# Blocks of 16 for the first three triangular inverses, joined by 32x32 products, and the norm products at another place in the later slots

## The chip, the cores and the metric

The kernel runs on one core of a Trainium2 chip. The metric is device time in microseconds (us) for one execution. The engines named here are TensorE (PE: matmuls; PEld: its weight loads), VectorE (DVE), ScalarE (ACT), GpSimd (POOL) and SyncE (SP). SP does no arithmetic; it issues DMA transfers in the order of its program, as POOL and ACT also do between their other instructions.

## The reference

Two blocks in a row. The first is a recurrence over 768 tokens for 4 x 8 heads with a 40 x 40 state each; the second is a feed-forward block with a softmax-weighted activation and a layer norm.

```python
for t in range(S):
    kt, vt, rt = (k[:, :, t], v[:, :, t], r[:, :, t])
    wt, at, bt = (w[:, :, t], a[:, :, t], b[:, :, t])
    y[:, :, t] = np.einsum('bhd,bhde->bhe', rt, state)
    Sa = np.einsum('bhde,bhe->bhd', state, at)
    state_decay = state * wt[:, :, None, :] - np.einsum('bhd,bhe->bhde', Sa, bt)
    state = state_decay + np.einsum('bhd,bhe->bhde', vt, kt)
...
h = x @ w_in
e = np.exp(h - h_max)
solu = h * (e / (np.sum(e, axis=-1, keepdims=True) + 1e-09))
ln = (solu - mu) / np.sqrt(var + 1e-06) * g_ln
out = ln @ w_out
```

Shapes: r, k, v, w, a, b are (4, 8, 768, 40) in float32; x is (3072, 320); w_in is (320, 1024) and w_out (1024, 320), both delivered in 64 bits and turned into float32 on the chip.

## The kernel before

The 768 tokens are cut into chunks of 64 (C), and two batches are worked on together, so there are 24 chunk steps i (N), each with 16 units (p, q, g, h) of one batch and head. Within a chunk the recurrence becomes products plus one triangular system per unit: a strictly triangular 64x64 matrix nt (line 383) has to be inverted as identity plus triangle. The kernel keeps two 32x32 diagonal blocks (Q = 32) of each and inverts them on VectorE; the off-diagonal block follows from two products on TensorE.

The inverse of two chunks (GRP = 2, so 32 units, 128 partitions with one block each) is one generator, `invert(n)` (line 402). `spread` (393) first reads the blocks back from a DRAM copy of nt into the tile blk. Then come 30 steps of forward substitution, each with one multiply (L415, prod) and one subtract (L417, uu) on VectorE. At the end the result is stored to DRAM (L422), and `bring(i)` (426) loads it in two arrangements: tu and uh. `flip` (438) transposes tu on VectorE, and `couple` (444, product py) and `close` (457, product pz) form the off-diagonal block.

The order of work is written out by hand for PE, POOL, DVE and SP; each of these engines runs its list in that order. The main loop (785) is a pipeline. One turn of it, called slot i here, starts at -1 and works on several chunks at once: the solution and output of chunk i (`driven`, `solved`, `answered`, `read`, `leave`), the preparation of chunk i+1 (`attend_kv`, `attend_rs`, `scores`, `couple`, `close`), `front`, `norm` and `scaled` of chunk j = i+5 and its neighbours, and the feed-forward block of earlier chunks (`hidden`, `exped`, `weighed`, `folded`, `output`). The steps of inverses are laid between these by `some(k)`, which advances the oldest inverse by k steps; the table `shares` (783) gives k for four places of a slot, and `narrowed` (784) says how many conversions of a weight part from 64 bits (`split`, 174: five VectorE and three ScalarE instructions) stand in the first and the second half of a slot. Ahead of the loop, chunks 0 to 3 pass through `front` and `norm`, inverse 0 is begun after chunk 1 and inverse 1 after chunk 3.

Names used below. nt is the masked product pnt of `norm`; psi and lv are the two masks of the product ps in `scores` (L505, L506, both recorded as L362); nmax (L655) is the row maximum with which the softmax chain begins; x and tot (L604, L619) are written by `leave`; kb is the scaled key tile on POOL (L329), and pb its transposition on TensorE; xT is the transposed activation that `leave` and `left` move by DMA on SP and POOL. Loads issued by `load_keys` and `load_values` go to SP unless another queue is given.

In slot i, TensorE's list runs: px (chunk i), pa, pb (chunk j), pu, pk, pv (chunk i+1), pnt (chunk j), pr, pst (chunk i+1), the last part of h, pei, pl, pcum, ps, py, pz, pyo.

Of the kernel before, what the change touches and what calls it, by code (L numbers as in the profile page):

```python
# [17 lines left out]
P = 128  # L18
# [4 lines left out]
AHEAD = 5  # L23
LANDS_NEXT = {2: 6, 3: 7, 5: 8, 6: 9, 7: 10, 8: 11, 10: 12}
LAG = 1
LN_EXP = "natural_log_exp_and_others"


def shape_constants():
    s, t = np.arange(P)[:, None], np.arange(P)[None, :]  # L30
    same = s // C == t // C
    row = np.arange(P)[:, None] % C
    parts = dict(
        ident=np.eye(P),
        cum=same & (s <= t),
        tri=row < np.arange(C)[None, :],
        eye_hi=row == Q + np.arange(Q)[None, :],
        neg_hi=-(row >= Q).astype(np.float64),
        mean=np.full((P, P), 2.0 ** -10),
    )  # L40
    at, where = 0, {}
    for name, x in parts.items():
        where[name] = (at, at + x.shape[1])
        at += x.shape[1]
    return np.concatenate([np.asarray(x, np.float64) for x in parts.values()], 1).astype(np.float32), where
# [3 lines left out]
def kernel(  # L49
# [46 lines left out]
    def c_(name):  # L96
        lo, hi = where[name]
        return cst[:, lo:hi]
# [8 lines left out]
    def zeroed(engine, name, shape, n, part=None):  # L107
        tiles = []
        for i in range(n):
            x = const.tile(shape, FP32, name=f"{name}{i}")  # L110
            engine.memset(x if part is None else part(x), 0.0)
            tiles.append(x)
        return tiles
# [10 lines left out]
    st_t = zeroed(nc.vector, "st", [P, 8, C], NPAIR)  # L124
    tu_t = zeroed(nc.vector, "tu", [P, H, 3 * Q], 2)
    uh_t = zeroed(nc.vector, "uh", [P, 2 * H, Q], 2)
    x0 = zeroed(nc.vector, "x", [P, 2, 4, C], 1, lambda x: x[:, :, :, D:])[0]
    wy = const.tile([P, 2, 4, C], FP32, name="wy")
    nc.vector.tensor_copy(out=wy.rearrange("p h j c -> p (h j) c")[:, :, Q:],
# [127 lines left out]
    def fence():  # L257
        nc.tensor.drain()
# [20 lines left out]
    def ok(i):  # L279
        return 0 <= i < N  # L280


    def load_keys(i, names, queue=nc.sync):
        if not ok(i):
            return
        for n, ap in (("w", w), ("b", b), ("a", a), ("k", k)):
            if n in names:
                x = a_t[i % 4] if n == "a" else two.tile([P, H, D], FP32, tag="raw_" + n, name="raw_" + n,
                                                             bufs=3)
                st[i]["raw_" + n] = x  # L290
                load(x, ap, i, queue)

# [80 lines left out]
    def norm(i):  # L373
        if not ok(i):
            return
        d = st[i]
        t = banks("pnt")
        for u in in_turn(lambda p, q, g, h: (h, p ^ h)):
            p, q, g, h = u
            j = 2 * q + g  # L380
            mm(t[half(p ^ h), h, j * C:j * C + C], keyed(d["bT"], u), keyed(d["aT"], u))
        nt = d["nt"] = tokens("nt", AHEAD)
        masked(nt, t[:, :, 0:256])
        n, at = divmod(i, GRP)
        if at == 0:
            blocks[n] = dram.tile([2 * GRP * H, C, C], FP32, tag="nt_dram", name="nt_dram")
        queue = nc.sync if i < 4 else nc.gpsimd
        queue.dma_start(out=blocks[n].rearrange("(a h x) s c -> a x s h c", a=GRP, x=2)[at].rearrange("x s h c -> (x s) h c"),  # L388
                          in_=nt.rearrange("p h j c -> p (h j) c"))
# [3 lines left out]
    def spread(n):  # L393
# [5 lines left out]
                queue.dma_start(out=nb[home:home + Q], in_=blocks[n][:, Q * e:Q * e + Q, Q * e:Q * e + Q])  # L399
        return nb  # L400

    def invert(n):
        nb = spread(n)
        yield
        u = two.tile([P, Q // 2, Q], FP32, tag="uu", name="uu")
        flat = u.rearrange("p c t -> p (c t)")
        nc.vector.memset(u[C:P], 0.0)
        nc.vector.memset(flat[C:P, 1::Q + 2], 1.0)
        nc.vector.tensor_scalar(out=u[0:C], in0=nb[0:C, 0::2], scalar1=-1.0, scalar2=None, op0=ALU.mult)
        nc.vector.memset(flat[0:C, 0::Q + 2], 1.0)  # L410
        for j in range(1, Q - 1):
            m, n_c = Q - 1 - j, (j + 1) // 2
            prod = two.tile([P, Q * Q // 8], FP32, tag="prod", name="prod", bufs=1)
            t = prod[:, 0:n_c * m].rearrange("p (c r) -> p c r", c=n_c)
            nc.vector.tensor_tensor(out=t, in0=nb[:, j:j + 1, j + 1:Q].to_broadcast([P, n_c, m]),  # L415
                                    in1=u[:, 0:n_c, j:j + 1].to_broadcast([P, n_c, m]), op=ALU.mult)
            nc.vector.tensor_tensor(out=u[:, 0:n_c, j + 1:Q], in0=u[:, 0:n_c, j + 1:Q], in1=t, op=ALU.subtract)  # L417
            if j < Q - 2:
                yield
        inverse[n] = dram.tile([C, Q, Q], FP32, tag="uu_dram", name="uu_dram")  # L420
        for y in range(2):
            nc.sync.dma_start(out=inverse[n][:, y::2], in_=u[C * y:C * y + C])  # L422
        yield


    def bring(i):
        if not ok(i):
            return
        d = st[i]
        d["tu"], d["uh"] = tu_t[i % 2], uh_t[i % 2]  # L430
        n, at = divmod(i, GRP)
        src = inverse[n].rearrange("(e a h x) c t -> e a h x c t", e=2, a=GRP, x=2)
        for x in range(2):
            nc.sync.dma_start(out=d["tu"][C * x:C * x + Q, :, Q:2 * Q], in_=src[0, at, :, x].rearrange("h c t -> c h t"))
        for x in range(2):
            nc.sync.dma_start(out=d["uh"][C * x + Q:C * x + C], in_=src[1, at].rearrange("h x c t -> c (h x) t"))

    def flip(i):
        if not ok(i):
# [273 lines left out]
    def some(n):  # L713
        while steps and n:
            if next(steps[0], steps) is steps:
                steps.pop(0)
            else:
                n -= 1
# [1 line left out]
    parts = ((n, part) for n in range(len(lands) + NF) for part in landed[n])  # L720

    def begin_inverse(n):
        steps.append(invert(n))
        next(steps[-1])


# [10 lines left out]
    for i in range(4):  # L737
        scaled(i, "b")
        if i == 3:
            scaled(0, "k")  # L740
            scaled(1, "k")
        front(i)
        decay(i + 1)
        norm(i)
        decay_turned(i + 1)
        if i == 0:
            load_keys(2, "ba")
        if i == 1:
            load_keys(3, "w")
            begin_inverse(0)  # L750
            narrow(2)
            load_keys(3, "ba")
            load_keys(0, "k")
            load_keys(4, "w")
            some(8)
        if i == 2:
            load_values(0)
            load_keys(1, "k")
            some(8)
    load_keys(5, "w")  # L760
    load_keys(4, "ba")
    begin_inverse(1)
    for i in (2, 3):
        load_keys(i, "k", nc.gpsimd)
# [5 lines left out]
    decay(5)  # L770
    load_keys(6, "w")
    land(3, nc.sync)
    some(14)
    load_keys(5, "ba")
    load_values(1)
    bring(0)
    bring(1)
    load_keys(5, "k")
    for n in (4, len(lands)):
        land(n, nc.sync)  # L780


    shares = {-1: (0, 6, 2, 6), 0: (0, 6, 4, 6), 1: (0, 6, 3, 6), 2: (0, 6, 3, 6), 3: (0, 6, 3, 6)}
    narrowed = {-1: (0, 1), 0: (1, 1), 1: (1, 2), 2: (1, 2), 3: (1, 1)}
    for i in range(-1, N + 3 + LAG):
        j, m = i + AHEAD, i - LAG
        pieces = shares.get(i, (3, 6, 0, 6))
        some_weights = narrowed.get(i, (0, 0))

        some(pieces[0])  # L790
        if i >= 1:
            bring(i + 1)
        if i >= 0:
            load_values(i + 2)
        carried(i)
        driven(i)
        front(j)
        hidden(m - 2, ((0, 1),))
        if i == 3 + LAG:
            centred(mean, 6)  # L800
        load_keys(j + 3, "w")
        load_keys(j + 2, "bak")
        narrow(some_weights[0], pieces[1])

        solved(i)
        attend_kv(i + 1)
        hidden(m - 2, ((1, 1),))
        norm(j)
        attend_rs(i + 1)
        hidden(m - 2, ((2, 0), (2, 1)))  # L810
        exped(m - 2)
        decay_turned(j + 1)
        scaled(j + 1)
        left(i - 1)

        answered(i)
        if i >= 0:
            flip(i + 1)
        weighed(m - 2)
        spreadof(m - 2)  # L820
        decay(j + 2)
        if i == 0:
            turn_g()
        if i == 2 + LAG:
            mean = mean_begun(6)
        output(m - 3, 0)
        if ok(j) and j % GRP == GRP - 1:
            begin_inverse(j // GRP)
        some(pieces[2])
        scores(i + 1)  # L830
        if i < 0:
            flip(i + 1)
        couple(i + 1)
        output(m - 3, 1)
        narrow(some_weights[1], pieces[3])

        close(i + 1)
        read(i, True)
        read(i, False)
        by_value(i + 2)  # L840
        leave(i)
        folded(m - 2)
        hidden(m - 1, ((0, 0), (1, 0)))
# [30 lines left out]
```

## Time and profile before

| what | value |
|---|---|
| time, median of 3 runs | 638.88 us (638.88 to 640.07) |
| the profiled execution, its own time | 639.79 us |
| its span in the profile | 637.7 us |
| mean granted TensorE clock | 0.93 |
| PE busy | 567.5 us (89%), 11451 instructions |
| DVE busy | 461.9 us (72%), 1286 instructions |
| ACT busy | 245.3 us (38%) |
| POOL busy | 269.1 us (42%) |
| L415 (prod), 360 instructions | 99.0 us, 275 ns each |
| L417 (uu), 360 instructions | 101.9 us, 283 ns each |
| chain that ended last, by engine | PE 71%, DVE 13%, DMA 6%, issue 4% |

The 360 steps belong to the twelve inverses. A float32 product shows as two weight loads and two matmuls in the records, which is why the counts there are twice those of the program. Busy time is the time in which an engine has an instruction running; a matmul's end is modelled, so its pace is better read from the starts of a series. The chain that ended last goes back from the last instruction, at each step to what released it.

### The profile page before, as it was taken

Reading aid. Unit: us, or ns where it says so; the run is one execution under the profiler, and the core shown is the slowest. Engines: PE = TensorE matmul, PEld = TensorE weight load, DVE = VectorE, ACT = ScalarE, POOL = GpSimd, SP = SyncE. Lnnn points to the kernel's source line nnn. Section 1 sums busy time; section 2 is a strip of 40 time slices with the busy share of each in tenths; the row PEclk is TensorE's granted clock in tenths of the full one; section 3 lists DMA queues with packets and bytes.
Section 4 is the critical chain, followed back from the end, with each engine's and each line's share of the span. In section 5 each row is a group of like instructions: output and inputs, shape, how many; then the busy total and the mean of one; then the engine's idle time right before and its main releaser. Section 6 shows DMA issues by size and latency. Waiting matters only on the chain.

```text
span 637.7 us, 26729 instructions
## 1 busy us (share of the span) xinstructions
PE 567.5 (89%) x11451; PEld 399.6 (63%) x11451; DVE 461.9 (72%) x1286; ACT 245.3 (38%) x498; POOL 269.1 (42%) x444
## 2 busy tenths in 40 slices
PE   5245677988999999999999999999999999999995
PEld 3134555756577677667667767666776666766653
DVE  4678799999878778778878777787887796443431
ACT  3412545554334434433443443344243333332221
POOL 3334345574274444445543642743544642222200
PEclk9665676688999999999999999999999999999998
DMA  8939896474355535544554553654423422210000
GB/s 166 159 73 169 170 164 131 107 152 87 71 110 93 111 87 95 107 93 103 103 120 79 108 116 73 119 107 95 91 53 70 98 49 49 51 36 26 24 20 21
DMA packets 217868, 59.92 MB, mean 94 GB/s; under 512 B 203216, under 2 KB 213048, under 8 KB 217752
## 3 DMA queue, kind: packets, MB, share of 16 engines
q1 hardware_dynamic: 200984, 34.47, 31.7%
q0 software_dynamic: 11376, 19.25, 12.6%
q10 hardware_dynamic: 5392, 4.51, 2.5%
q8 instruction: 90, 1.47, 1.0%
q14 instruction: 26, 0.21, 0.1%
HBM read 40.10 MB, written 13.37 MB: 84 GB/s over the span
## 4 chain that ended last, share of the span: by engine, by line
PE 71%; DVE 13%; DMA 6%; issue 4%; ACT 2%; SPq 2%; POOL 1%; DVEq 0%; ACTq 0%; POOLq 0%
PE h L254 16%; PE po L703 14%; PE pyo L254 7%; PE px L254 4%; PE pu L254 3%; DVE uu L417 3%; PE plnT L692 3%; PE ps L254 3%; DVE prod L415 3%; PE pl L254 2%; PE pr L334 2%; PE pnt L254 2%; PE pk L334 2%; PE pa L334 2%; PE pz L254 2%
## 5 line engine op out<-in xcount | busy, mean ns | idle before, releaser
L254 PE MATMUL h<-w_in,xT 128*128 128x512 f32 (+1 forms) x288 | 121.6, 614 | 0.0
L415 DVE TENSOR_TENSOR prod<-blk,uu 128x30 f32<-128x30 f32 (+4 forms) x360 | 99.0, 275 | 24.0 <-DMA blk<-nt_dram 14.0
L703 PE MATMUL po<-w,lnT 128*128 128x320 f32 x384 | 113.5, 440 | 0.0
L417 DVE TENSOR_TENSOR uu<-uu,prod 128x30 f32<-128x30 f32 (+4 forms) x360 | 101.9, 283 | 12.4
L703 PEld LDWEIGHTS po<-w,lnT 128*128 128x128 f32 x384 | 70.5, 190 | 29.3 <-issue 2.3
L655 DVE TENSOR_REDUCE nmax<-h 128x1 f32<-128x1024 f32 x24 | 29.4, 1224 | 60.0 <-PE h L254 59.9
L388 POOL DMA_DIRECT2D nt_dram<-nt x20 | 18.3, 916 | 119.0 <-DVE nt L362 97.7
L254 PEld LDWEIGHTS h<-w_in,xT 128*128 128x128 f32 (+1 forms) x288 | 38.9, 190 | 21.9 <-issue 20.8
L623 POOL TENSOR_TENSOR st<-tot,ex 104x160 f32<-104x160 f32 x44 | 22.1, 520 | 70.4 <-DVE tot L619 68.2
L681 POOL TENSOR_TENSOR rs<-c,mhalf 128x1 f32<-128x1 f32 x24 | 13.4, 559 | 91.0 <-DVE c L680 89.6
L635 POOL DMA_DIRECT2D xT<-x x96 | 48.7, 512 | 0.0
L254 PE MATMUL pyo<-lv,kb 64*64 64x104 f32 x768 | 38.6, 274 | 6.0 <-DVE lv L362 3.3
L693 ACT COPY lnT<-plnT 128x512 f32<-128x512 f32 x48 | 26.1, 589 | 43.3 <-PE plnT L692 43.3
L399 POOL DMA_DIRECT2D blk<-nt_dram x42 | 33.3, 800 | 13.0 <-DMA nt_dram<-nt 12.7
L658 ACT ACTIVATE e<-h,nmax 128x1024 f32<-128x1024 f32 x24 | 26.8, 1115 | 28.6 <-DVE nmax L655 27.5
L254 PE MATMUL pyo<-lu,kb 64*64 64x104 f32 x768 | 37.2, 266 | 0.0
L664 DVE TENSOR_TENSOR e<-h,e 128x1024 f32<-128x1024 f32 x24 | 29.4, 1225 | 10.1 <-ACT e L658 10.1
L276 POOL DMA_DIRECT2D raw_r<-in_r_dram x48 | 34.9, 729 | 0.3 <-issue 0.3
L672 DVE BATCH_NORM_STATS2 bs<-e 128x6 f32<-128x512 f32 x48 | 30.9, 686 | 0.8
L707 ACT ACTIVATE osb<-po,rs 128x320 f32<-128x320 f32 x24 | 12.7, 528 | 48.5 <-PE po L703 29.6
L254 PEld LDWEIGHTS pnt<-aT,bT 40*64 40x64 f32 x768 | 14.6, 144 | 26.5 <-issue 25.0
L254 PEld LDWEIGHTS pyo<-lv,kb 64*64 64x64 f32 x768 | 23.9, 145 | 11.3 <-issue 7.7
(130 smaller groups left out, 1127.0 us busy)
## 6 DMA issues: line engine op xcount, KB each, us to landing
blk<-nt_dram POOLq DMA_DIRECT2D x42, 128.0 KB, 4.2
nt_dram<-nt POOLq DMA_DIRECT2D x20, 256.0 KB, 3.5
raw_w<-in_w_dram SPq DMA_DIRECT2D x48, 80.0 KB
a<-in_a_dram SPq DMA_DIRECT2D x48, 80.0 KB
raw_r<-in_r_dram POOLq DMA_DIRECT2D x48, 80.0 KB, 3.3
lv<-in_v_dram SPq DMA_DIRECT2D x48, 80.0 KB
out_dram<-osb ACTq DMA_DIRECT2D x24, 160.0 KB
raw_b<-in_b_dram SPq DMA_DIRECT2D x44, 80.0 KB
```

What stands on the lines that cost most here:

```text
L254: nc.tensor.matmul(o, lhsT=lhsT, rhs=rhs, start=start, stop=stop, skip_group_check=True)
L276: queue.dma_start(out=x[half(p), :, 0:D], in_=ap[2 * bp + p, :, ci * C:(ci + 1) * C, :].rearrange("h t d -> t h d"))
L334: nc.tensor.transpose(out=t[0:W2, j * P:(j + 1) * P], in_=x[:, 2 * j:2 * j + 2].rearrange("p a b -> p (a b)")[:, 0:W2], identity=ident)
L399: queue.dma_start(out=nb[home:home + Q], in_=blocks[n][:, Q * e:Q * e + Q, Q * e:Q * e + Q])
L415: nc.vector.tensor_tensor(out=t, in0=nb[:, j:j + 1, j + 1:Q].to_broadcast([P, n_c, m]), in1=u[:, 0:n_c, j:j + 1].to_broadcast([P, n_c, m]) ...
L417: nc.vector.tensor_tensor(out=u[:, 0:n_c, j + 1:Q], in0=u[:, 0:n_c, j + 1:Q], in1=t, op=ALU.subtract)
L635: nc.gpsimd.dma_start(out=xT[to:to + Q, 2], in_=x[at + P - 3 * D:at + D, 2])
L655: nc.vector.tensor_reduce(out=nmax, in_=d["h"], axis=AX.X, op=ALU.max, negate=True)
L658: nc.scalar.activation(out=e, in_=d["h"], func=AF.Exp, bias=nmax, accum_out=d["esum"])
L664: nc.vector.tensor_tensor(out=d["e"], in0=d["h"], in1=d["e"], op=ALU.mult)
L672: nc.vector.bn_stats(out=bs[:, x], in_=d["e"][:, x * 512:x * 512 + 512])
L703: nc.tensor.matmul(d["out"][:, 0:DM], lhsT=d["lnT"][:, f, :], rhs=w2[:, f, :], start=f == 0, stop=f == NF - 1)
```

## The change

For the inverses n = 0, 1, 2 (chunks 0 to 5; `SMALL = 3`) a new generator `invert_small` inverts diagonal blocks of 16 (`R = 16`) instead of 32. All 128 partitions hold one such block: four a unit, 32 units. It needs 14 steps. The result goes to DRAM, and `bring` loads it with eight DMAs a chunk into a tile e16 (for odd and later chunks four of the eight are on POOL). A new function `joined(i)` makes blocks of 32 from it: VectorE transposes e16 (f16), 32 products of 32x32 with 16 columns give pw, VectorE turns this into v16, and 2 x 16 products give pe, which ScalarE copies in six pieces into tu and uh. From there on all is as before. `joined(i + 1)` stands in the slot between `norm` and `attend_rs`.

For slots from 4 on, `norm(j)` is moved behind `answered(i)`. `shares` and `narrowed` have other numbers in slots -1 to 3, one conversion of a weight part is moved ahead of the loop, loads of chunks 4 and 5 and `bring(0)` are moved ahead of chunk 3, two of the four blk loads of inverse 1 are on POOL, and raw_k has two buffers instead of three.

```diff
+SMALL = 3
+R = 16
...
-                                                             bufs=3)
+                                                             bufs=2 if n == "k" else 3)
...
+    def invert_small(n):
+        nb = two.tile([P, Q, Q], FP32, tag="blk", name="blk").rearrange("p a b -> p (a b)")[:, 0:R * R]
+        nb = nb.rearrange("p (c t) -> p c t", c=R)
+        for y in range(4):
+            queue = nc.gpsimd if n > 1 or y > 1 else nc.sync
+            queue.dma_start(out=nb[Q * y:Q * y + Q], in_=blocks[n][:, R * y:R * y + R, R * y:R * y + R])
+        yield
+        flat = two.tile([P, Q // 2, Q], FP32, tag="uu", name="uu").rearrange("p c t -> p (c t)")[:, 0:R * R]
+        u = flat.rearrange("p (c t) -> p c t", c=R)
+        nc.vector.tensor_scalar(out=u, in0=nb, scalar1=-1.0, scalar2=None, op0=ALU.mult)
+        nc.vector.memset(flat[:, 0::R + 1], 1.0)
+        for j in range(1, R - 1):
+            step(nb, u, j, j, R)
+            if j < R - 2:
+                yield
+        inverse[n] = dram.tile([P, R, R], FP32, tag="small_dram", name="small_dram")
+        nc.sync.dma_start(out=inverse[n], in_=u)
+        yield
...
+        if n < SMALL:
+            src = inverse[n].rearrange("(y a h x) c t -> y a h x c t", y=4, a=GRP, x=2)
+            for y in range(4):
+                for x in range(2):
+                    (nc.gpsimd if x and i else nc.sync).dma_start(
+                        out=e_t[i % 2][C * x + R * y:C * x + R * y + R, :, R * (y % 2):R * (y % 2) + R],
+                        in_=src[y, at, :, x].rearrange("h c t -> c h t"))
+            return
...
+    def joined(i):
...
+        nc.vector.transpose(out=f16, in_=e)
+        t = bank("pw")
+        for n, (y, x) in enumerate(((0, 0), (0, 1), (1, 0), (1, 1))):
+            if n:
+                fence()
+            for u in on(x):
+                mm(t[block(x, y), R * at(u):R * at(u) + R], d["nt"][block(x, y), u[3], 2 * u[1] + u[2], Q * y:Q * y + Q],
+                   f16[block(x, y), at(u), 0:R])
+        nc.vector.scalar_tensor_tensor(out=v16[:, :, 0:R], in0=t[:, 0:H * R].rearrange("p (u c) -> p u c", u=H), scalar=c_("neg_r"),
+                                       in1=c_("eye_l").unsqueeze(1).to_broadcast([P, H, R]), op0=ALU.mult, op1=ALU.add)
+        for y in range(2):
+            t = bank("pe")
+            for x in range(2):
+                if x:
+                    fence()
+                for u in on(x):
+                    mm(t[block(u[0] if y else x, y), Q * at(u):Q * at(u) + Q], v16[block(x, y), at(u)], e[block(x, y), at(u)])
...
+                    nc.scalar.copy(out=d["tu"][block(x, 0), :, Q:2 * Q], in_=t[block(x, 0)])
...
+                    nc.scalar.copy(out=d["uh"][block(x, 1), 2 * 4 * h + (x ^ h):2 * 4 * h + 8:2], in_=t[block(x, 1), 4 * h:4 * h + 4])
...
-            some(8)
+            some(7)
         if i == 2:
             load_values(0)
             load_keys(1, "k")
-            some(8)
-    load_keys(5, "w")
-    load_keys(4, "ba")
+            some(7)
+            load_keys(5, "w")
+            load_keys(4, "ba")
+            bring(0)
     begin_inverse(1)
...
     land(3, nc.sync)
-    some(14)
+    narrow(1)
+    bring(1)
     load_keys(5, "ba")
     load_values(1)
-    bring(0)
-    bring(1)
...
-    shares = {-1: (0, 6, 2, 6), 0: (0, 6, 4, 6), 1: (0, 6, 3, 6), 2: (0, 6, 3, 6), 3: (0, 6, 3, 6)}
-    narrowed = {-1: (0, 1), 0: (1, 1), 1: (1, 2), 2: (1, 2), 3: (1, 1)}
+    shares = {-1: (0, 5, 3, 6), 0: (0, 0, 0, 0), 1: (0, 4, 2, 3), 2: (0, 3, 1, 1), 3: (0, 6, 3, 6)}
+    narrowed = {-1: (0, 1), 0: (1, 1), 1: (1, 2), 2: (1, 2), 3: (1, 0)}
...
-        norm(j)
+        if i < 4:
+            norm(j)
+        joined(i + 1)
         attend_rs(i + 1)
...
         answered(i)
+        if i >= 4:
+            norm(j)
```

`fence()` is TensorE's drain. `step` is the old pair of multiply and subtract as a function.

More of the change, by code (lines that the diff above doesn't have):

```diff
@@ L39, in shape_constants @@
         mean=np.full((P, P), 2.0 ** -10),
+        eye_l=np.arange(P)[:, None] % Q == np.arange(R)[None, :],
+        eye_r=np.arange(P)[:, None] % Q == R + np.arange(R)[None, :],
+        neg_r=-(np.arange(P)[:, None] % Q >= R).astype(np.float64),
     )
@@ L126 @@
     uh_t = zeroed(nc.vector, "uh", [P, 2 * H, Q], 2)
+    e_t = zeroed(nc.gpsimd, "e16_", [P, H, Q], 2)
+    f16 = const.tile([P, H, Q], FP32, name="f16")
+    v16 = const.tile([P, H, Q], FP32, name="v16")
+    nc.vector.tensor_copy(out=v16[:, :, R:], in_=c_("eye_r").unsqueeze(1).to_broadcast([P, H, R]))
     x0 = zeroed(nc.vector, "x", [P, 2, 4, C], 1, lambda x: x[:, :, :, D:])[0]
@@ L400, in spread, with step @@
         return nb
+    def invert_small(n):
[16 more added lines that the diff above has]
+        yield
+    def step(nb, u, j, n_c, size):
+        m = size - 1 - j
+        prod = two.tile([P, Q * Q // 8], FP32, tag="prod", name="prod", bufs=1)
+        t = prod[:, 0:n_c * m].rearrange("p (c r) -> p c r", c=n_c)
+        nc.vector.tensor_tensor(out=t, in0=nb[:, j:j + 1, j + 1:size].to_broadcast([P, n_c, m]),
+                                in1=u[:, 0:n_c, j:j + 1].to_broadcast([P, n_c, m]), op=ALU.mult)
+        nc.vector.tensor_tensor(out=u[:, 0:n_c, j + 1:size], in0=u[:, 0:n_c, j + 1:size], in1=t, op=ALU.subtract)
     def invert(n):
@@ L411, in invert @@
         for j in range(1, Q - 1):
[L412 to L417, printed above, removed]
+            step(nb, u, j, (j + 1) // 2, Q)
             if j < Q - 2:
@@ L436, in bring @@
             nc.sync.dma_start(out=d["uh"][C * x + Q:C * x + C], in_=src[1, at].rearrange("h x c t -> c (h x) t"))
+    def joined(i):
+        if not ok(i) or i // GRP >= SMALL:
+            return
+        d = st[i]
+        e = e_t[i % 2]
+        on = lambda x: [u for u in units if u[0] ^ u[3] == x]
+        at = lambda u: 4 * u[3] + 2 * u[1] + u[2]
+        block = lambda x, y: slice(C * x + Q * y, C * x + Q * y + Q)
+        nc.vector.transpose(out=f16, in_=e)
[15 more added lines that the diff above has]
+                    mm(t[block(u[0] if y else x, y), Q * at(u):Q * at(u) + Q], v16[block(x, y), at(u)], e[block(x, y), at(u)])
+            t = t[:, 0:H * Q].rearrange("p (u c) -> p u c", u=H)
+            for x in range(2):
+                if not y:
+                    nc.scalar.copy(out=d["tu"][block(x, 0), :, Q:2 * Q], in_=t[block(x, 0)])
+                    continue
+                for h in range(2):
+                    nc.scalar.copy(out=d["uh"][block(x, 1), 2 * 4 * h + (x ^ h):2 * 4 * h + 8:2], in_=t[block(x, 1), 4 * h:4 * h + 4])
     def flip(i):
@@ L722, in begin_inverse @@
     def begin_inverse(n):
-        steps.append(invert(n))
+        steps.append((invert_small if n < SMALL else invert)(n))
         next(steps[-1])
```

## Prediction

> **What bounds the kernel now.** I read the page's slices first, then stretches of the span in a table of windows, then the order of time on each engine. In the slices each digit is a fortieth of the span, in tenths busy.
>
> ```profile
> PE   5245677988999999999999999999999999999995
> DVE  4678799999878778778878777787887796443431
> PEclk9665676688999999999999999999999999999998
> ```
>
> TensorE (PE) is full from slice 10 (some 160 us) to 600 us. Before that VectorE (DVE) is the fuller engine, and the clock granted to TensorE is low. The windows (length, then busy time and instructions of PE, PEld, DVE, ACT, POOL; clock; DMA share; GB/s) say the same:
>
> ```profile
> 60.00:70.00 10.00, 6.35 (x110) 4.72 (x106) 6.14 (x20) 3.81 (x8) 1.77 (x2) 0.50 0.75 133
> 80.00:90.00 10.00, 5.41 (x194) 4.35 (x196) 9.65 (x22) 3.57 (x11) 3.92 (x5) 0.88 0.88 162
> 300.00:350.00 50.00, 49.45 (x1106) 34.83 (x1105) 38.52 (x111) 19.50 (x41) 23.63 (x39) 1.00 0.51 101
> ```
>
> From 160 us on nothing but TensorE work counts, and the later slots (22.5 us each while inverses run) follow from the moment the early ones end. So I price the early slots only. I mark them by the start of the psi mask of chunk i, which closes slot i-1: T0 to T5. The timeline of VectorE gives them (start, duration, engine, line):
>
> ```profile
> 66.38 0.69 DVE L362 TENSOR_TENSOR psi<-ps,cst 128x512 f32<-128x512 f32 x1 [3.45 <-PE ps L254]
> ...
> 82.08 0.69 DVE L362 TENSOR_TENSOR nt<-pnt,cst 128x512 f32<-128x512 f32 x1
> ...
> 87.50 0.68 DVE L362 TENSOR_TENSOR psi<-ps,cst 128x512 f32<-128x512 f32 x1
> ```
>
> T0 = 66.4, T1 = 87.5, and further on T2 = 108.2, T3 = 129.3, T4 = 154.45, T5 = 180.3. Slots 0 to 2 take 21 us because VectorE works through inverse steps and weight conversion without a pause; slots 3 and 4 take 25.
>
> [...] the trace has no 32x32 products, but its drain between the two px groups costs 0.11 us.
>
> **The change part by part.**
>
> **Steps taken out.** A 32-step costs two VectorE instructions of 0.19 to 0.29 us; small ones are not much cheaper, since the fixed part decides:
>
> ```profile
> 30.24 0.19 DVE L415 TENSOR_TENSOR prod<-blk,uu 128x30 f32<-128x30 f32 x1 [1.41 <-DMA blk<-nt_dram]
> 31.14 0.22 DVE L415 TENSOR_TENSOR prod<-blk,uu 128x56 f32<-128x56 f32 x1
> ```
>
> With the hand-over a new step (14 to 56 columns) is about 0.47 us, an old one 0.56. Thirty old ones are 16.8 us, fourteen new ones 6.5: VectorE loses 10 us per inverse, 31 us for three.
>
> **Products put in (`joined`), six times.** In TensorE's order they stand between pnt and pr. VectorE's part (f16, then v16) stands behind nt, so behind all the narrowing and steps of the first half slot. All of r, ei, pl, scores of the slot wait behind them. Price J from the start of f16 to TensorE going on: f16 0.44 (the row of tu, L442, same shape); v16 0.28 (a mask of 128x128); five drains 0.55; three hand-overs 0.3; 64 products. A product of 32x32 is not in the trace. From below: 16 products 64x64, taken in turn over four tiles, take 0.62 us, 39 ns each. From above: each tile then makes a product in 4 x 39 = 155 ns, and here eight in a row lie on one tile, but with half the columns. I take 60 ns: 3.8 us. J = 5.4 us; at 39 ns 4.1, at 155 ns 11.5.
>
> **Up to T0.** VectorE starts the inverse at about 28; seven steps (3.3), aT, nt(2) by 34; seven more end at 37.4, six or so microseconds before the old nt(3). But SP now issues, ahead of the nt(3) store: lv, raw_k(1), the small store (37.4), raw_w(5), raw_b(4), a(4) (1.3 us a pair: 41.8), then eight e16 loads. At 0.45 us each, with the last waiting for a(4), they end about 45.4. So the store goes out as late as before:
>
> ```profile
> 45.76 0.38 SPq L388 DMA_DIRECT2D nt_dram<-nt  x1
> ...
> 44.11 2.72 POOL L276 DMA_DIRECT2D raw_k<-in_k_dram  x4
> ...
> 52.12 0.86 POOL L329 TENSOR_TENSOR kb<-raw_b,inv 128x320 f32<-128x320 f32 x1 [1.17 <-DMA raw_b<-in_b_dram]
> ```
>
> And two of the four blk loads of inverse 1 are now on POOL, ahead of the raw_k loads, where they wait for that store to land (3.5 us: 49). Then 1.8 + 0.6 for them, and the 6.9 us of work that lay between 44.11 and 52.12 (its wait taken off) bring kb(4) to 58.2 instead of 52.1. So pb(4) is at 59.2 (54.6 before), pk, pv, pnt follow at the half clock, nt(4) ends at 63.9 (61.9). Then joined(0), partly at the half clock: 7.5 (4.1 to 13), and pr, pei, pcum, ps: 4.3 (3.2 at the full clock, 5.4 at the half). T0 = 75.7, +9.3 (+5 to +16).
>
> **Slot 0.** nt(5) ended at T0 + 16.4. Twelve large steps (7.4) go, six small (2.8) come, and the second narrowing, with no steps inside it, waits 1.7 for ScalarE: 13.5, less 0.4 for the stall of a slow conversion: f16 at 13.1. Then J 5.4, then pr, pei, pl, pcum, ps (0.5, 0.9 with the wait for its bank, 0.6, 0.8, 1.1 in the rows of slot 0) 3.9: 22.4 against 21.1, +1.3. Before, after nt only 5.4 us were left to the next mark, so what VectorE saves (3 us) is less than what TensorE's chain adds.
>
> **Slot 1.** VectorE is at f16 by about 12.1. But e16 for chunk 2 is issued behind xT of leave: x at T1 + 5.6, four xT issues 3.4 (95.39 to 98.8 in SP's queue before), four e16 2.0, landing 2.2: 13.2. Then J and 4.3 (pst is added): 22.9 against 20.7, +2.2. Before, tu and uh came the same way, but flip needed them only late.
>
> **Slot 2.** Two conversions stand ahead of x (T2 + 9.2 as before): e16 lands at 16.8. With J and 4.3: 26.5 against 21.1, +5.4.
>
> **Slot 3.** Here the inverses are of 32 again and VectorE saves nothing: nt(8) ends at T3 + 17.05 as before. Then the softmax chain follows, which needs all of h, and the last h products now stand behind `joined`.
>
> ```profile
> 145.78 0.68 DVE L362 TENSOR_TENSOR nt<-pnt,cst 128x512 f32<-128x512 f32 x1
> 146.38 1.21 DVE L655 TENSOR_REDUCE nmax<-h 128x1 f32<-128x1024 f32 x1
> ```
>
> After: 17.05 + 5.4, pr, pst and h 2.1, so nmax at 24.6 instead of 17.05; the 8.1 us from nmax to the mark stay. +7.5.
>
> **Slot 4.** f16 takes nt's place at T4 + 19.2; + 5.4 + 2.1 = 26.7 for nmax instead of 20.2; nt (0.6) comes behind it: +7.1.
>
> **From slot 4 on, norm behind answered.** The same 16 products; nt comes 3.5 us later, but POOL issued the blk loads only at 315.88, behind rs, and the store still lands by then. 0, at most 0.1 us a slot: -2 to +2. raw_k with two buffers: a load then waits for the kb of two chunks before, done a slot earlier, 0. The extra conversion ahead of the loop lies before kb(4): 0. ScalarE's six copies a chunk (1.7 us, busy 38%) hide under pe and pr, except 0.3 counted in the 3.9 and 4.3.
>
> Sum: 9.3 + 1.3 + 2.2 + 5.4 + 7.5 + 7.1 = 32.8. Span 637.7 becomes 670.5; the profiled execution took 639.8 and the median is 638.9, 1.2 over the span: 671.7, and I say 671.
>
> **The rivals.** On the other side, VectorE's relief gets through and the kernel is faster. For it: VectorE is 90% busy and TensorE idle 57 us before 170. If TensorE could do `joined` in idle time, with f16 early, the stage would shrink by VectorE's 31 less six times 0.72 (26.7), and only slots 3 and 4 would pay, 5.4 each: 623. It decides if f16 starts at or before T + 8 in slots 0 to 2, by 5 us earlier than I count. Against it: f16's place behind nt and the narrowing in VectorE's own order. 8%; no change 2%.
>
> A mild case: the start costs nothing and chunks 2 and 3 find their loads. The POOL wait falls into idle time and e16 is in time; then T0 and slots 0 to 2 come out even, and slots 3 and 4 pay their TensorE time: 638.9 + 11 = 650. Against it: kb(4) is on the chain to pnt(4). 16%.
>
> A dear case: products on one tile are slow. At 110 ns instead of 60, and at half clock in the waits, J is 8.6 or more, six times 3.2: 671 + 19 = 690, up to 708. For it: f16 leaves TensorE idle about 4 us in slots 0 to 2. 14%.
>
> My forecast has 60%, by itself 658 to 685 (39 ns and a mild start below; 80 ns above).
>
> **How the numbers follow.** Three runs spread 0.2%, so about 1.3 us is what can be told from no change. The range takes in my own case and most of the two slower rivals: 649 to 692; it leaves out the faster case and the upper half of the dear products. Faster 0.08, same 0.02, slower 0.90.
>
> **What would show it.** Right: the kb(4) row on POOL near 58 with a wait for nt_dram ahead of it; psi marks 20 to 22 us apart turning into 22 to 34; waits of f16 for e16 loads in slots 1 and 2; nmax waiting for h in slots 3 and 4. Wrong: `pw` and `pe` at 39 ns or less with f16 early, T0 at or under 67, or TensorE gaps in the later slots that the moved norm closes.

## The result and the profile after

The changed kernel takes 702.64 us (median of 4 runs, 699.47 to 705.1) against 638.88: 1.0991 times as long, 95% interval 1.0939 to 1.1042. It is slower, as forecast, but by 63.8 us instead of 32, and outside the range. The profiled execution is the fastest of its four, 699.47 us with a span of 697.7, so views are compared by spans: 697.7 against 637.7, 60.0 more.

The page's slices of the changed kernel (TensorE, VectorE, clock granted to TensorE):

```profile
PE   5243877859697989999999999999999999999995
DVE  4752425353475459889898888888888778434432
PEclk9655666677778799999999999999999999999998
```

VectorE is relieved indeed: from the fourth slice to the fourteenth it fell from 7 to 9 tenths to between 2 and 5, once 7. (A slice is 17.4 us now and was 15.9.) TensorE is not fuller for it: in these slices it has 3 to 9 tenths where it had 5 to 9, and its clock is at 5 to 8 tenths from the second slice to the fourteenth. The windows of slots 0 and 4 (length; busy time and instructions of PE, PEld, DVE, ACT, POOL; clock; DMA share; GB/s) put sizes to it, first of the kernel before, then of the changed one:

```profile
66.38:87.50 21.12, 12.84 (x379) 10.56 (x379) 20.01 (x49) 10.12 (x23) 7.63 (x10) 0.82 0.95 174
...
154.45:180.28 25.83, 22.87 (x449) 16.41 (x450) 21.94 (x56) 9.77 (x20) 8.11 (x13) 0.93 0.34 65
```

```profile
79.80:107.18 27.38, 20.63 (x456) 17.20 (x459) 12.07 (x31) 11.66 (x29) 8.47 (x12) 0.68 0.38 69
...
203.21:241.92 38.71, 32.43 (x604) 23.79 (x596) 20.90 (x54) 10.10 (x23) 10.27 (x17) 0.78 0.20 36
```

In slot 0 VectorE has 12 us of work in 27.4, where it had 20 in 21.1; TensorE is busy for 20.6 of them at 0.68 of its clock. In slot 4 TensorE is busy for 32.4 instead of 22.9, at 0.78 instead of 0.93. The marks, read from the psi masks in VectorE's timeline:

| | T0 | slot 0 | slot 1 | slot 2 | slot 3 | slot 4 | T5 |
|---|---|---|---|---|---|---|---|
| before | 66.38 | 21.12 | 20.72 | 21.11 | 25.12 | 25.83 | 180.28 |
| after | 79.80 | 27.38 | 28.53 | 30.47 | 37.03 | 38.71 | 241.92 |
| longer by | 13.4 | 6.3 | 7.8 | 9.4 | 11.9 | 12.9 | 61.6 |
| forecast | 9.3 | 1.3 | 2.2 | 5.4 | 7.5 | 7.1 | 32.8 |

After T5 the changed kernel gains 1.6 us. How a slot loses its time is seen in slot 3, in TensorE's timeline of the changed kernel (start, duration, what; a float32 product shows as two records):

```profile
183.38 4.32 PE L263 MATMUL pw<-f,nt 32*32 32x16 f32 x64 [4.10 <-DVE f L488]
188.19 1.03 PE L263 MATMUL pe<-e,v 32*32 32x32 f32 x16 [0.49 <-issue]
189.41 1.29 PE L263 MATMUL pe<-e,v 32*32 32x32 f32 x32 [0.19 <-DMA xT<-x]
190.91 0.65 PE L263 MATMUL pe<-e,v 32*32 32x32 f32 x16 [0.20 <-issue]
191.49 1.09 PE L343 MATMUL pr<-cst,r 128*104 128x128 f32 x4
...
193.55 2.08 PE L263 MATMUL h<-w_in,xT 64*128 64x512 f32 x4
```

TensorE waits 4.10 us for f16, then takes 4.32 us for the 32 products of pw and 3.30 (188.19 to 191.49) for the 32 of pe: 119 ns each with their drains. With f16 (from 182.79) and v16 that is J = 8.70 us. Then pr and h take almost twice as long as in the same slot of the kernel before:

```profile
143.31 0.64 PE L334 MATMUL pr<-cst,r 128*104 128x128 f32 x4
...
144.32 1.13 PE L254 MATMUL h<-w_in,xT 64*128 64x512 f32 x4
```

The granted clock of the changed kernel is 0.50 from the start of pw (183.38) to 195.6, and 1.00 after it. VectorE's timeline shows who pays; the softmax maximum needs that last h:

```profile
195.68 1.23 DVE L730 TENSOR_REDUCE nmax<-h 128x1 f32<-128x1024 f32 x1 [7.59 <-PE h L263]
```

At 195.68, 29.5 us after the slot's start, stands what in the kernel before stood at 17.05.

J was 7.74, 8.33, 8.70, 8.69, 8.70 and 8.69 us in the six places. Up to T0 there is POOL besides, whose timeline shows the blk loads standing ahead of the raw_k loads and of kb of chunk 4 (the last line):

```profile
50.58 1.32 POOL L418 DMA_DIRECT2D blk<-nt_dram  x2 [8.38 <-DMA nt_dram<-nt]
51.89 2.71 POOL L285 DMA_DIRECT2D raw_k<-in_k_dram  x4
...
61.44 0.86 POOL L338 TENSOR_TENSOR kb<-raw_b,inv 128x320 f32<-128x320 f32 x1
```

### The profile page after: what moved, and what is told of

It reads as the page before. It is cut to its first block, busy times and chain, and to the rows that moved or that the text cites. A ratio compares the mean times of both kernels' runs of the same rounds, so it can differ in the third digit from the quotient of the medians.

```text
span 697.7 us, 28295 instructions
## 1 busy us (share of the span) xinstructions
PE 606.0 (87%) x12219; PEld 433.9 (62%) x12219; DVE 451.5 (65%) x1197; ACT 255.2 (37%) x534; POOL 280.8 (40%) x468
## 4 chain that ended last, share of the span: by engine, by line
PE 69%; issue 8%; DMA 8%; POOL 4%; DVE 4%; SPq 4%; ACT 1%; DVEq 0%; POOLq 0%; ACTq 0%
PE h L263 15%; PE po L778 14%; PE pyo L263 6%; PE px L263 3%; PE ps L263 3%; PE plnT L767 3%; PE pu L263 3%; SPq L285 2%; PE pl L263 2%; PE pz L263 2%; PE pr L343 2%; PE pei L343 2%; PE pcum L326 2%; PE pw L263 2%; PE pe L263 2%
## 5 line engine op out<-in xcount | busy, mean ns | idle before, releaser
L436 DVE TENSOR_TENSOR prod<-blk,uu 128x54 f32<-128x54 f32 (+10 forms) x312 | 101.8, 326 | 13.0 <-DMA blk<-nt_dram 4.3
L438 DVE TENSOR_TENSOR uu<-uu,prod 128x54 f32<-128x54 f32 (+10 forms) x312 | 88.9, 285 | 10.7
L730 DVE TENSOR_REDUCE nmax<-h 128x1 f32<-128x1024 f32 x24 | 29.4, 1225 | 69.5 <-PE h L263 69.5
L756 POOL TENSOR_TENSOR rs<-c,mhalf 128x1 f32<-128x1 f32 x24 | 13.4, 560 | 117.4 <-DVE c L755 117.4
L698 POOL TENSOR_TENSOR st<-tot,ex 104x160 f32<-104x160 f32 x44 | 23.2, 545 | 69.2 <-DVE tot L694 68.9
L263 PE MATMUL pw<-f,nt 32*32 32x16 f32 x384 | 23.1, 205 | 20.6 <-DVE f L488 19.1
L263 PE MATMUL pyo<-lv,kb 64*64 64x104 f32 x768 | 36.9, 264 | 2.6
L263 PE MATMUL pyo<-lu,kb 64*64 64x104 f32 x768 | 35.7, 257 | 0.0
L263 PEld LDWEIGHTS pw<-f,nt 32*32 32x32 f32 x384 | 20.9, 143 | 23.7 <-issue 23.7
L343 PE MATMUL pb<-cst,kb 128*104 128x128 f32 x96 | 16.7, 303 | 18.8 <-POOL kb L338 18.5
L739 DVE TENSOR_TENSOR e<-h,e 128x1024 f32<-128x1024 f32 x24 | 28.8, 1200 | 6.0 <-ACT e L733 6.0
L371 DVE TENSOR_TENSOR lu<-pl,cst 128x512 f32<-128x512 f32 x24 | 16.5, 689 | 22.1 <-PE pl L263 22.1
```

The lines of the kernel that those rows point to most:

```text
L263: nc.tensor.matmul(o, lhsT=lhsT, rhs=rhs, start=start, stop=stop, skip_group_check=True)
L343: nc.tensor.transpose(out=t[0:W2, j * P:(j + 1) * P], in_=x[:, 2 * j:2 * j + 2].rearrange("p a b -> p (a b)")[:, 0:W2], identity=ident)
L436: nc.vector.tensor_tensor(out=t, in0=nb[:, j:j + 1, j + 1:size].to_broadcast([P, n_c, m]), in1=u[:, 0:n_c, j:j + 1].to_broadcast([P, n_c, ...
L438: nc.vector.tensor_tensor(out=u[:, 0:n_c, j + 1:size], in0=u[:, 0:n_c, j + 1:size], in1=t, op=ALU.subtract)
L730: nc.vector.tensor_reduce(out=nmax, in_=d["h"], axis=AX.X, op=ALU.max, negate=True)
L739: nc.vector.tensor_tensor(out=d["e"], in0=d["h"], in1=d["e"], op=ALU.mult)
```

## The experiments

The theory after the result: the loss is `joined`, by three things: the price of a small product, a clock that the wait for f16 and the small products take away (during J and after it), and the place of `joined`, ahead of what VectorE waits for. Rivals: the start and the order of the loads; a fixed price of a small product wherever it lies; idle time alone as the cause of the clock. The kernel before ran beside each group of runs, at 639.03, 640.72 and 639.92 us; ratios are against these, and microseconds gained are against the changed kernel's 702.64.

**Products in turn over the tiles.**

```diff
-        for n, (y, x) in enumerate(((0, 0), (0, 1), (1, 0), (1, 1))):
-            if n:
-                fence()
-            for u in on(x):
-                mm(t[block(x, y), R * at(u):R * at(u) + R], d["nt"][block(x, y), u[3], 2 * u[1] + u[2], Q * y:Q * y + Q],
+        turns = in_turn(lambda p, q, g, h: (p ^ h, p))
...
+        for y in range(2):
+            if y:
+                fence()
+            for u in turns:
+                x = u[0] ^ u[3]
+                mm(t[block(x, y), x, R * at(u):R * at(u) + R], d["nt"][block(x, y), u[3], 2 * u[1] + u[2], Q * y:Q * y + Q],
                    f16[block(x, y), at(u), 0:R])
```

(The same for pe, without a drain; t has two banks.)

> The changed kernel with its 32x32 products taken in turn over the tiles (two tiles in pw and in the first half of pe, four in the second half; one more bank for the second group of rows, v16 in two halves), so that no product follows another on the same tile. Same products, same place. Theory 'a tile takes about 150 ns for a product and others may run beside it': in the changed kernel's trace two tiles in turn took 75 ns a product, so pw falls from 4.5 to about 2.5 us, pe from 3.6 to about 1.8, J from 8.7 to about 5 us, six times 3.6 = 21 us: 681 us. Theory 'each small product costs TensorE a fixed time wherever it lies, the half clock is the reason': J stays at 8.5 to 9.5, 700 to 706 us.

Measured: 680.38 us, ratio 1.0643 (1.0626 to 1.066): 22.3 less than the changed kernel. J is 4.84 to 4.94 us in five places and 4.13 in the sixth, slot 4. In TensorE's timeline of this run, slots 3 and 4:

```profile
172.15 2.17 PE L263 MATMUL pw<-f,nt 32*32 32x16 f32 x64 [3.13 <-DVE f L488]
...
206.77 1.46 PE L263 MATMUL pw<-f,nt 32*32 32x16 f32 x64 [2.48 <-DVE f L488]
...
210.41 1.09 PE L343 MATMUL pr<-cst,r 128*104 128x128 f32 x4
```

In slot 3 the same 32 products of pw take 2.17 us instead of 4.32, both at a clock of 0.50. In slot 4 they take 1.46 at 1.00; in a row on one tile they take 2.92 at that clock (next run). So the clock is not what halves them, and the rival of a fixed price wherever a product lies falls; the price is that of products in a row on one tile: 91 ns each at 1.00, where two tiles in turn take 46. Four of the five drains go with the new order, which the prediction put at 0.11 us each. Six times about 3.7 us is the whole gain.

**TensorE busy while f16 is made.**

```diff
         t = bank("pw")
+        for n in range(28):
+            nc.tensor.transpose(out=t[:, P * (n % 4):P * (n % 4) + P], in_=ident, identity=ident)
+        fence()
```

> The changed kernel with 28 transposes of the identity (128x128) put in TensorE's order ahead of pw, into the bank that pw then writes over: TensorE is busy for some 3 us of the 2.6 to 4.5 us that it otherwise waits for f16. Nothing of the result changes. Theory 'the wait for f16 takes the clock away': the clock stays up, pr and what follows J go back from about 1.07 to 0.5-0.6 us each, J falls to 6 or 7 us, and the time falls by 10 to 25 us, to 678-692. Theory 'the small products themselves count as idle': pw and pe may begin fast, but pr still takes 1.07, the time stays within 698 to 708. Where f16 is no longer waited for (slot 4), the filling itself costs up to 1 us.

Measured: 696.8 us, ratio 1.0906 (1.0877 to 1.0936), 5.8 less. Slot 4 in TensorE's timeline (the first line is part of the filling):

```profile
218.81 2.56 PE L491 MATMUL pw<-cst 128*128 128x128 f32 x22
221.45 2.92 PE L263 MATMUL pw<-f,nt 32*32 32x16 f32 x64
...
227.57 1.09 PE L343 MATMUL pr<-cst,r 128*104 128x128 f32 x4
...
229.63 2.08 PE L263 MATMUL h<-w_in,xT 64*128 64x512 f32 x4
```

Both theories get half. The wait did take the clock from pw: in slot 4 of the changed kernel pw takes 4.32 us at 0.50, here, with the wait filled, 2.92 us, 91 ns a product, and J is 7.28 in slot 4 (6.76 in slot 3, 7.06 in slot 1; 8.1 to 10.4 in the other three, where the filling ended too late or the clock was still low). Over these 2.92 us the clock was 1.00. But by pr it is at 0.50 again (pr takes 1.09 us, as in the changed kernel), though TensorE never paused for longer than 0.5 us from the filling on.

**Without joined.** `joined` returns at once.

> The changed kernel without joined: f16, v16, the 64 products and six copies of each of chunks 0 to 5 are left out, so that these chunks' inverse blocks stay zero. Everything else (the start, the 16-step inverses, the e16 loads, the moved norm) stays. Theory 'the loss is joined in its place': all of slots 0 to 4 comes back and VectorE's relief shows, 702.6 less six times 8.7 and 11 us of half clock after it, and some of the waits: 625 to 640 us, T0 still about 72. Theory 'a good part is the start and the order of loads': 650 to 665.

Measured: 630.02 us, ratio 0.9859 (0.9842 to 0.9877). The whole loss, and 9 us more, goes with `joined` and with what waits for it. T0 is 68.9, only 2.5 later than before, though POOL and SP have the order of loads of the changed kernel and kb of chunk 4 comes as late (60.98). The window of slot 1 without joined:

```profile
84.12:99.43 15.31, 12.25 (x422) 9.89 (x414) 12.37 (x35) 9.89 (x21) 11.91 (x21) 1.00 0.58 129
```

It takes 15.3 us instead of 20.7, at the full clock, and slot 0 takes 15.2 instead of 21.1: VectorE's relief is real. It does not come through everywhere: slot 3 takes 29.4 us instead of 25.1, and there, near the start, TensorE waits for ScalarE:

```profile
120.92 1.08 PE L263 MATMUL pz<-uh,wy 64*64 64x32 f32 x32 [3.41 <-ACT wy L528]
```

**The blk loads of the second inverse on SP.**

```diff
-            queue = nc.gpsimd if n > 1 or y > 1 else nc.sync
+            queue = nc.gpsimd if n > 1 or y > 1 and not n else nc.sync
```

> The changed kernel with the blk loads of the second inverse all on SP's queue, so that POOL doesn't stand waiting for the nt store ahead of the raw_k loads and kb(4). Theory 'POOL's place sets T0': kb(4) comes at 53 to 56 instead of 61.4, T0 at 73 to 75 instead of 79.8, the time 4 to 7 us less, 696 to 699. Theory 'nt(4) is late for another reason (raw_k or the clock)': T0 at 78 to 80, 701 to 704 us.

Measured: 694.23 us, ratio 1.0856 (1.0817 to 1.0894), 8.4 less. T0 falls to 70.12, by 9.7. In POOL's timeline of this run the same kb comes 12 us earlier than in the changed kernel:

```profile
49.44 0.86 POOL L338 TENSOR_TENSOR kb<-raw_b,inv 128x320 f32<-128x320 f32 x1
```

More than expected: the wait held the raw_k loads for 10 us (51.89 against 41.71), not only kb. Slot 0 gives 3.1 us back, because f16 then comes at T0 + 15.1 instead of T0 + 12.3, and slots 1 and 3 give back 1.2 and 1.4. What the order of the loads costs thus depends on `joined` behind it: with `joined` it makes T0 9.7 us later, while without `joined` T0 was only 2.5 us later than in the kernel before.

**Joined behind answered.**

```diff
-        joined(i + 1)
         attend_rs(i + 1)
...
         answered(i)
+        joined(i + 1)
```

> The changed kernel with joined(i+1) moved down behind answered(i), so that pr, pei, pl and the last h products of the slot stand ahead of pw in TensorE's order, and f16 behind the softmax chain's VectorE work. The products, and their 8.7 us, stay. Theory 'place counts: what stands behind joined is late by J': nmax in slots 3 and 4 no longer waits (7.6 us each), TensorE does 2 to 3 us of useful work while f16 is made, lu comes earlier; ps and so the psi mark still follow J. Slots 3 and 4 lose about 7 us each, slots 0 to 2 about 2 each: 680 us, between 672 and 688. Theory 'only the price of J counts, wherever it stands': 697 to 704.

Measured: 684.82 us, ratio 1.0681 (1.0656 to 1.0706), 17.8 less; place counts. In VectorE's timeline of this run nmax has no wait, in slot 3 18.65 us after the slot's start (157.44):

```profile
176.09 1.22 DVE L730 TENSOR_REDUCE nmax<-h 128x1 f32<-128x1024 f32 x1
```

But slot 3 became only 1.5 us shorter and slot 4 only 5.2, less than the 7 each that I expected; slots 0 to 2 gained 2.2, 2.6 and 2.1. In slot 3 what remains is TensorE's: pw 3.86 us, and what follows at about half speed (pcum 1.44 us instead of 0.81).

**Edits together.** First: in turn, and blk on SP.

> The changed kernel with products in turn over the tiles and the blk loads of the second inverse on SP, joined at its place. Additive: 702.6 - 22.3 - 8.4 = 672. If the earlier T0 is eaten by the e16 loads of slots 1 and 2: 676 to 680.

Measured: 670.3 us, ratio 1.0456 (1.0417 to 1.0494): they add up. Then joined behind answered as well:

> The changed kernel with three edits together: products in turn over the tiles (22 us gained alone), blk loads of the second inverse on SP (8 alone), joined behind answered. If the three take away different waits: 702.6 - 22 - 8 - 20 = 652. If the late place and the cheaper products take away the same us: 665 to 672. Under 639, so faster than the kernel before, only if J then lies wholly beside VectorE's work.

Measured: 659.09 us, ratio 1.0281 (1.0252 to 1.0309). Added up, the three gains (22.3, 8.4, 17.8) would give 654.1, so about 5 us of them overlap. T0 is then 66.18, as before the change, but slots 3 and 4 take 32.1 and 32.7 us against 25.1 and 25.8.

**Norm alone, in the kernel before.** Only `norm(j)` is moved as in the change.

> The kernel before with nothing but norm's products moved behind answered from slot 4 on; inverses as before. Forecast: the products are the same and the store still lands in time: 0, -2 to +2, so 637 to 641 with 639 the likeliest. Theory 'h and the softmax chain come earlier by pnt's 1.6 us and later slots shrink': the changed kernel lost 1.6 us less by the end than at T5, so 637.3. Theory 'the inverses of later slots wait for their blk loads': 641 to 645.

Measured: 637.61 us, ratio 0.9951 (0.9932 to 0.997). It is the one version here that does all the work and takes less time than the kernel before. Why is in the last section.

**A dose of small products where nothing is waited for.** The kernel of the last run gets 64 products of 32x32 by 32x16, whose results nobody reads, in six slots of its steady part. A function `dosed` places them ahead of the slot's last h products; its number is that of the tiles they go over in turn (1 is eight in a row on one tile, then a drain):

```diff
+        dosed(i, {6: 1, 7: 1, 9: 2, 10: 2, 12: 4, 13: 4}.get(i, 0))
         hidden(m - 2, ((2, 0), (2, 1)))
```

> The kernel before with norm moved (637.6 us), and besides, in six steady slots where TensorE is full and waits for nothing, 64 products of 32x32 by 32x16 whose results nobody reads: in slots 6 and 7 eight in a row on one tile, in 9 and 10 in turn over two tiles, in 12 and 13 over four. The lengthening of each slot over 22.2 us is the price without any wait for f16. From the filled run (91 ns a product on one tile at the full clock) and the late one (46 ns over two tiles): 5.8, 3 and 1.5 to 3 us of products. Theory 'small products themselves bring the clock down': the windows of slots 6 and 7 show a clock under 1.00, what follows runs at twice its time for some 4 us, and the slots grow by 7 to 8, 4.5 to 5 and 2.5 to 4 us: about 668 us. Theory 'only idle time does': the clock stays 1.00, the slots grow by 5.8, 3 and 1.5 to 2: about 658 us.

Measured: 667.67 us, ratio 1.0429 (1.0398 to 1.046). Against 22.2 us the slots grew by 8.3 and 8.1 (one tile), 3.8 and 5.6 (two), 1.9 and 1.7 (four). TensorE's timeline in slots 6, 10 and 13 of this run:

```profile
219.41 6.59 PE L254 MATMUL pw<-cst,nt 32*32 32x16 f32 x128
225.93 2.08 PE L254 MATMUL h<-w_in,xT 64*128 64x512 f32 x4
...
328.47 2.66 PE L254 MATMUL pw<-cst,nt 32*32 32x16 f32 x128
331.06 1.13 PE L254 MATMUL h<-w_in,xT 64*128 64x512 f32 x4
332.12 1.09 PE L334 MATMUL pei<-cst,ei 128*104 128x128 f32 x4
...
402.87 1.58 PE L254 MATMUL pw<-cst,nt 32*32 32x16 f32 x128
404.38 1.16 PE L254 MATMUL h<-w_in,xT 64*128 64x512 f32 x4
```

The windows of the products of slot 6 and of what follows them:

```profile
219.00:226.00 7.00, 6.51 (x135) 5.72 (x133) 0.78 (x4) 1.07 (x2) 0.00 (x0) 0.78 0.61 102
226.00:230.00 4.00, 4.00 (x52) 2.13 (x56) 1.23 (x1) 0.88 (x2) 0.00 (x0) 0.53 0.00 0
```

64 products take 6.5, 2.6 and 1.5 us: 102, 40 and 24 ns each. TensorE waited for no other engine, and yet on one tile the h behind them takes 2.08 us instead of 1.13, in both slots. The clock falls while the products run: in slot 6 it is 1.00 in their first 3.2 us and 0.55 in the rest, so the 102 ns are not a price at the full clock. Over two tiles the clock fell in slot 10, after the products, and not in slot 9 (windows of 5 us behind the products: 0.52 and 1.00), where the series had a pause of 0.94 us in it and took 3.75 us in all; over four it stayed (1.00 behind both doses). So three of the six doses, two of 6.4 and 6.6 us on one tile and one of 2.7 us over two, were followed by work at half speed although TensorE was kept busy. The rival that only idle time does so falls. With more tiles the series is also shorter and has fewer drains; which of these keeps the clock up the run does not tell apart.

**Four tiles, and fewer small inverses.** Both with joined behind answered. First all three inverses, and pw and pe over four tiles each (two pairs of banks, v16 in four parts):

> As the run with three edits (turn, late, blk on SP), with the products in turn over four tiles in pw and pe alike, no drain between, and v16 in four parts. Theory 'a tile's own time is the price': J falls from 4.3 by 0.5 to 1.3 us, six times: 651 to 656. Theory 'over two tiles TensorE's issue is already the limit': 658 to 661.

Measured: 655.78 us, ratio 1.0254 (1.022 to 1.0287). That is 3.3 us less than over two tiles, but the intervals of the two ratios overlap (1.0252 to 1.0309 there), so it is not clear of noise. J fell by 0.2 us on average and not by the 0.5 to 1.3 expected: 4.0 to 4.6 us against 4.1 to 5.1, since v16 in four parts takes 1.45 us instead of 0.73. In slot 2 of this run TensorE's timeline shows what is left:

```profile
129.16 0.74 PE L263 MATMUL pw<-f,nt 32*32 32x16 f32 x64 [1.18 <-DVE f L488]
131.23 1.61 PE L263 MATMUL pe<-e,v 32*32 32x32 f32 x64 [1.33 <-DVE v L499]
132.77 1.44 PE L326 MATMUL pcum<-lw,cst 128*128 128x320 f32 x2
```

The products cost 2.35 us now, the waits for f16 and v16 take 2.5, and what follows is at half speed still (pcum 1.44; 0.81 in a late slot). Then two, and one:

> The same, with only the first two inverses of 16 and the third of 32 as before (its 30 steps in slots 1 and 2 as before). Theory 'slots 3 and 4 are bound by TensorE and pay all of joined': these slots come back from 32 to 25-26 us, slots 1 and 2 stay near 22 to 25: 641 to 648. Theory 'VectorE's relief in slots 1 and 2 is worth as much': 652 to 660.

> The same with only the first inverse of 16 (chunks 0 and 1), the other two of 32 as before. Theory 'no dose pays: each inverse costs TensorE two J and gives VectorE 10 us where TensorE is then late': 638 to 644, not under the 637.6 of norm's move alone. Theory 'the first one, where VectorE is the fuller engine, pays': 630 to 636.

Measured: 647.6 us (1.0126, 1.0102 to 1.015) and 646.42 us (1.0113, 1.0078 to 1.0149; here the blk loads of the second inverse are as in the kernel before). Slots 3 and 4 of the first came back to 26.0 and 26.4. With none there are 637.61 (ratio 0.9951), so no number of small inverses pays in this arrangement; these runs keep the changed order of loads too. The second is above what I expected: T0 and slot 0 cost 2.1 and 4.5 us more than with norm moved alone, and slots 3 and 4, which have no joined there, 1.7 and 1.0 more. Why those two are longer I did not find.

## Why the prediction was right and where it was wrong

**The term that failed: the price of a product in J.** "I take 60 ns: 3.8 us. J = 5.4 us." The products and their drains take 7.6 us (4.32 + 3.30) where the prediction had 4.35 (3.8 + 0.55): J came out 2.9 us longer than 5.4 in slot 0 and 3.3 in each of slots 1 to 4, 16.1 us up to T5. The prediction cut the upper bound of 155 ns, read off 64x64 products, to 60 because there are half the columns; this was too much credit. In a row on one tile, drains included, a product of pw takes 91 ns at the full clock (the filled run) and 135 at half (4.32 us for 32), so at least 1.4 of the 3.3 us are the clock in pw. 40 to 46 ns, near the lower bound of 39, came only where the products went in turn over two tiles at the full clock.

**The term that was missing: the half clock behind joined.** What follows J was priced from rows of the kernel before: 3.9 and 4.3 us up to the next mark, 2.1 up to nmax. Measured from the start of pr: 6.7, 6.4 and 6.6 us in slots 0 to 2, 4.2 and 4.2 to nmax in slots 3 and 4, 5.2 instead of 4.3 at T0: 12.2 us together. In these stretches TensorE was busy without a pause (33.1 of 33.2 us), at a clock of 0.50 to 0.62. The prediction counted half clock only up to T0, and took the products for work that keeps the clock up; that was its estimate, and no trace had shown it. Nor did its own window 60:70 show a low clock only behind long waits: the clock was 0.50 there, with TensorE busy for 6.35 of 10 us and no wait longer than 1.9 us since 51.39. The two terms together are 28.3 us of the 28.8 by which the forecast fell short at T5. The rest is small only because other errors cancel: nt(4) was 3.0 us later than forecast, and f16 in the slots 2.3 us earlier in sum.

**Up to T0: the mechanism was right.** POOL stood 8.38 us before its blk loads, and kb of chunk 4 came at 61.4, not 58.2; nt(4) ended at 66.95, not 63.9. The store that POOL waits for left SP at 47.72 and not as early as before (45.76), and an earlier kb then waited 2.06 us for its raw_k load, which the prediction, with the waits taken off, put at nothing. The run with the loads on SP shows what POOL's order costs: 12 us for kb and, with `joined` behind it, 9.7 for T0.

**The starts of f16 were nearly right.** From the last mark: 12.3, 13.5, 15.2, 16.6 and 19.5 us in slots 0 to 4, where 13.1, 13.2, 16.8, 17.05 and 19.2 were forecast. The waits for the e16 loads in slots 1 and 2 came, at 1.06 and 1.03 us. The largest miss is 1.6 us. So it was right that f16 stands behind nt and the narrowing and that in this order of work VectorE's relief does not bring it to T + 8.

**Norm's move at 0** was wrong: the prediction counted "at most 0.1 us a slot: -2 to +2". It saves 0.3 us a slot, and the ratio of 0.9951 is 3.1 us, beyond the -2.

**The rivals.** What came is the dear case, which I gave 14%: "At 110 ns instead of 60, and at half clock in the waits, J is 8.6 or more", 690 to 708. The line spoken for it, that f16 leaves TensorE idle about 4 us, was true (2.6 to 4.5). The sum of 690 leaves out the half clock behind `joined` as well. For the faster kernel the prediction read VectorE as 90% busy before 170; that holds from T0 to T5 (104.1 of 113.9 us), while before 170 it is 137.4 us, 81%. The case is not empty: without `joined` there are 630 us. But it needs `joined` in TensorE's idle time, and no run here reached it, not even with four tiles and a better place.

## What to carry to other kernels

Work taken from VectorE and given to TensorE in small tiles needed two prices here: that of products that follow each other on one tile (91 ns at the full clock, 135 at half), and that of the dense work behind them at the clock that they left (h 2.08 us instead of 1.13). Small products cost less in turn over several tiles (22.3 us gained over two; four, in the late place, gave 3.3 more, within noise) and behind what other engines wait for (17.8 us). And two blk loads that waited in POOL's order, ahead of loads that the next stage needed, held all of them: POOL stood 8.38 us, and with the two on SP kb came 12 us and T0 9.7 us earlier.

## What the runs showed of the hardware

The clock fell during small products while TensorE was busy: over 64 products in 6.5 us on one tile, with TensorE busy for 6.5 of the 7.0 us of the window above, it went from 1.00 to 0.55. Of the two doses over two tiles one was followed by 0.52 and the other by 1.00; they differ by the pause of 0.94 us, and why only one lost the clock was not shown. The cost behind the dose of slot 6: h, pei and pl at about half speed for 3.9 us (225.93 to 229.82; 2.08, 1.09 and 1.03 us, where behind the dose of slot 13 they take 1.16, 0.65 and 0.69).

Series of one tile shape took less time side by side. With norm moved, pnt stands behind pl, both recorded as 40*64; before, it stood between h and pr. TensorE's timeline in a late slot, first of the kernel before, then with norm moved:

```profile
306.74 0.69 PE L254 MATMUL pnt<-aT,bT 40*64 40x64 f32 x32
307.36 0.64 PE L334 MATMUL pr<-cst,r 128*104 128x128 f32 x4
...
310.01 0.69 PE L254 MATMUL pl<-rT,nuT 40*64 40x64 f32 x32
310.64 0.81 PE L317 MATMUL pcum<-lw,cst 128*128 128x320 f32 x2
```

```profile
310.67 0.69 PE L254 MATMUL pl<-rT,nuT 40*64 40x64 f32 x32
311.19 0.65 PE L254 MATMUL pnt<-aT,bT 40*64 40x64 f32 x32
311.76 0.81 PE L317 MATMUL pcum<-lw,cst 128*128 128x320 f32 x2
```

From start to start, pnt and pl took 0.62 + 0.63 us and take 0.52 + 0.57; with 0.10 saved between h and pr it is 0.26 a slot, and the slots went from 22.48 to 22.19. That it is the change of tile shape which costs the 0.1 us was not tried by itself.
